# Storing the results of a fused attention and spectral-mix kernel: last rows by another queue, pair tiles by one DMA of two blocks

## The chip, the cores and the metric

One core of one Trainium2 chip. The metric is the device time of one execution, in microseconds (us); medians of several executions are quoted.

## The reference, cut to what matters

Windowed causal attention over 8 batches of 576 positions gives x (8, 576, 512). A spectral mix transforms x along the positions, multiplies 64 modes by complex weights and transforms back to y. The output is u + relu(u @ w_ch) with u = x + y, in float32: 9.44 MB.

```python
X = np.fft.rfft(x, axis=1)
Yr = einsum(Xr, w_r) - einsum(Xi, w_i); Yi = einsum(Xr, w_i) + einsum(Xi, w_r)   # 64 modes
y = np.fft.irfft(Y, n=S, axis=1)
u = x + y
return (u + np.maximum(u @ w_ch, 0.0)).astype(np.float32)
```

## The kernel before

576 rows are 4 tiles of 128 rows and one of 64. The 64 last rows of two batches share a tile of 128 partitions, the pair tile; there are four. Two whole tiles of a batch are stored together, as 128 descriptors of 4 KB (two output rows per partition). The inverse transform of batch b multiplies a table with that batch's spectrum rows (`Y`); 8 of those rows come last of all, are computed for batches 2 to 7 in one tile (`yl`), and are moved by DMA into partitions 120 to 127 of the batch's own tile.

```python
def send(b):                                    # the last 8 rows of batch b
    r0 = 2 * R + RL * (b - 2)
    nc.sync.dma_start(out=batch_tile(b)[128 - RL:].bitcast(FP32), in_=yl[r0:r0 + RL].bitcast(FP32))
...
def finish(n):                                  # last product, sum and store of tile n
    b, t = seq[n]
    add(n, "Yb", True)
    ...
    nc.vector.tensor_tensor(out=ot[:, j], in0=ps, in1=x_sb[:, b, t, :], op=ALU.add)
    if t == NT - 1:                             # the pair tile: two halves
        for i, queue in enumerate((nc.sync, nc.sync)):
            queue.dma_start(out=out[b + i, 128 * t:, :], in_=ot[64 * i:64 * i + 64, 0])
    ...
    elif j:                                     # two whole tiles
        nc.sync.dma_start(out=out[b, 128 * t - 128:128 * t + 128, :].rearrange("(p j) e -> p j e", j=2), in_=ot)
...
send(2)
turn_of = {1: 3, 3: 4, 5: 5, 7: 6, 8: 7}
for n in range(NQ):
    finish(n)
    if n in turn_of:
        send(turn_of[n])
    ...                                         # products and rectification of later tiles
```

The softmax here doesn't subtract the row's maximum and nothing guards it: scores larger than these inputs give would overflow.

## Time and profile before

| what | kernel before |
|---|---|
| time, median of 5 | 430.04 us (429.55 to 430.32) |
| last weight transfer to the first row transfer | 391.2 to 397.1 us of the span |
| stores, first packet to last | 399.2 to 426.1 us |
| VectorE's last sum ends | 420.4 us |
| span | 427.3 us |

The part to look at is small: 31 us of 427. An average over the span (DMA engines over 90% busy) says nothing about it, because the weight stream fills the rest. One reads the last slices, then stretches of some us within them, then the sync queue's own timeline. The prediction shows those lines. A packet there is one record of a DMA engine's work: one contiguous run of up to 4 KB, or a 4-byte semaphore write.

### The profile page before, as it was taken

To read this page: it belongs to the slowest core of one execution; us is meant where nothing else is said; L and a number is where in the kernel's file an instruction comes from. 1 tells how busy PE (TensorE), PEld (TensorE's weight loads), DVE (VectorE), ACT (ScalarE), POOL (GpSimd) and SP (SyncE) were. 2 spreads that over 40 slices of the span, in tenths; PEclk is the share of its full clock that TensorE was granted. 3 is DMA by queue.
4 is the path that set the end of the run, shared out by engine and by line. 5 is a ranking of instruction groups with operands and counts; after the bars stand their busy time and mean duration, and the time that the engine had idled before them with its cause. 6 is when DMAs were issued, how large, how long until landed. Compare 5 with 4: busy or idle time off the path is not lost.

```text
span 427.3 us, 11629 instructions
## 1 busy us (share of the span) xinstructions
PE 322.1 (75%) x5179; PEld 230.8 (54%) x5186; DVE 176.1 (41%) x372; ACT 164.1 (38%) x290; POOL 89.4 (21%) x171
## 2 busy tenths in 40 slices
PE   6989998998998866422488877876367685498992
PEld 5755765765665566411367666654245452266781
DVE  5566765765764200306223332221113332141993
ACT  4585765866863221001022322222012221131991
POOL 7231231241112232211221221221111122100000
PEclk9999998999996655555588998899556965589997
DMA  7999999999999999999999999999999999993698
GB/s 142 212 213 213 213 212 213 214 211 214 214 213 213 214 213 261 214 214 213 213 213 215 213 212 214 214 214 213 212 215 213 214 213 214 214 214 68 219 351 333
DMA packets 28721, 92.16 MB, mean 216 GB/s; under 512 B 2896, under 2 KB 3152, under 8 KB 28672
## 3 DMA queue, kind: packets, MB, share of 16 engines
q0 software_dynamic: 25344, 81.80, 96.1%
q1 hardware_dynamic: 3184, 9.50, 6.0%
q8 instruction: 40, 0.66, 0.6%
q10 hardware_dynamic: 144, 0.13, 0.1%
q14 instruction: 9, 0.07, 0.0%
HBM read 162.53 MB, written 9.44 MB: 402 GB/s over the span
## 4 chain that ended last, share of the span: by engine, by line
DMA 51%; PE 32%; DVE 8%; issue 4%; ACT 2%; POOL 1%; DVEq 0%; POOLq 0%
DMA wt<-in_moe_w_i_dram 45%; PE pso L316 7%; PE pst L218 6%; DMA wy<-in_moe_w_i_dram 4%; PE pso L859 4%; PE psv L235 3%; DVE x_sb L324 3%; PE pss L372 3%; PE pss L272 2%; DMA wt<-in_moe_w_r_dram 2%; PE psx L338 2%; PE pss L291 2%; DVE vT L59 2%; PE psw L709 1%; DVE ot L882 1%
## 5 line engine op out<-in xcount | busy, mean ns | idle before, releaser
L563 PE MATMUL psy<-XQ,wt 128*128 128x16 bf16 x1616 | 61.4, 191 | 72.8 <-DMA wt<-in_moe_w_i_dram 37.6
L563 PEld LDWEIGHTS <-wt 128*128 128x128 bf16 x1616 | 53.2, 103 | 87.5 <-DMA wt<-in_moe_w_i_dram 42.4
L591 DVE CAST xT<-pxt 128x256 fp32r<-128x256 bf16 (+1 forms) x68 | 26.1, 434 | 61.8 <-PE pxt L584 39.4
L115 POOL DMA_DIRECT2D wt<-in_moe_w_r_dram x54 | 29.0, 537 | 87.8 <-DMA wt<-in_moe_w_r_dram 42.2
L596 ACT CAST Z<-psz 128x512 fp32r<-128x512 f32 x36 | 21.1, 586 | 66.9 <-PE psz L594 66.6
L115 POOL DMA_DIRECT2D wt<-in_moe_w_i_dram x52 | 27.9, 536 | 84.7 <-DMA wt<-in_moe_w_i_dram 53.7
L594 PE MATMUL psz<-wch,xT 128*128 128x512 f32 x144 | 45.3, 457 | 0.0
L297 ACT ACTIVATE et<-pss 128x512 bf16<-128x512 f32 x72 | 39.2, 599 | 13.2 <-PE pss L291 13.2
L316 PE MATMUL pso<-vt,et 128*64 128x65 bf16 (+1 forms) x576 | 34.3, 210 | 5.2 <-DVE x_sb L324 5.1
L316 PEld LDWEIGHTS <-et 128*64 128x64 bf16 (+1 forms) x576 | 23.9, 114 | 17.3 <-issue 9.8
L594 PEld LDWEIGHTS psz<-wch,xT 128*128 128x128 f32 x144 | 29.2, 217 | 5.8 <-ACT Z L596 0.4
L324 DVE TENSOR_TENSOR x_sb<-pso,rcp 128x640 bf16<-128x640 f32 x32 | 26.3, 822 | 0.9
L859 PE MATMUL pso<-Y,trigI 128*128 128x512 f32 x80 | 23.1, 402 | 0.1
L59 DVE CAST YT<-psy 128x256 fp32r<-128x256 f32 x6 | 2.5, 423 | 49.4 <-PE psy L563 49.4
L882 DVE TENSOR_TENSOR ot<-pso,x_sb 128x512 f32<-128x512 f32 x35 | 22.2, 685 | 1.5 <-PE pso L859 1.1
L59 DVE CAST x_sb<-psj 128x512 bf16<-128x512 f32 x16 | 11.0, 688 | 27.2 <-PE psj L771 27.1
L58 ACT CAST YT<-psy 128x256 fp32r<-128x256 f32 x6 | 2.2, 373 | 50.7 <-DVE YT L59 50.7
L272 PE MATMUL pss<-band,ident_bf 64*64 64x512 bf16 x136 | 20.5, 414 | 1.5 <-ACT et L297 1.5
L59 DVE COPY vT<-pst 128x768 bf16<-128x768 bf16 x16 | 15.3, 957 | 13.0 <-PE pst L218 13.0
L58 ACT CAST x_sb<-psj 128x512 bf16<-128x512 f32 x16 | 9.4, 586 | 26.9 <-PE psj L771 26.9
L864 ACT ACTIVATE pso<-pso 128x512 f32<-128x512 f32 x36 | 19.1, 597 | 0.0
L859 PEld LDWEIGHTS pso<-Y,trigI 128*128 128x128 f32 x80 | 14.5, 188 | 5.5 <-ACT pso L864 1.7
(158 smaller groups left out, 496.3 us busy)
## 6 DMA issues: line engine op xcount, KB each, us to landing
wt<-in_moe_w_r_dram POOLq DMA_DIRECT2D x54, 512.0 KB, 19.1
wt<-in_moe_w_i_dram POOLq DMA_DIRECT2D x52, 512.0 KB, 19.1
out_dram<-ot SPq DMA_DIRECT2D x15, 512.0 KB, 4.2
rk<-in_k_dram POOLq DMA_DIRECT2D x8, 576.0 KB, 9.0
rq<-in_q_dram POOLq DMA_DIRECT2D x8, 576.0 KB, 12.9
rv<-in_v_dram POOLq DMA_DIRECT2D x8, 576.0 KB, 11.9
wy<-in_moe_w_r_dram POOLq DMA_DIRECT2D x3, 512.0 KB, 16.9
wy<-in_moe_w_i_dram POOLq DMA_DIRECT2D x3, 512.0 KB, 19.1
```

Source lines behind the costliest of these rows:

```text
L59: return nc.vector.tensor_copy(out=o, in_=i)
L115: nc.gpsimd.dma_start(out=wt, in_=src[m].rearrange("(p c) e -> p c e", c=NC))
L218: nc.tensor.transpose(out=ps[64 * hh:64 * hh + 64, c, :], in_=src[:, hh, (c0 + c) * D:(c0 + c + 1) * D], identity=ident_bf)
L272: nc.tensor.matmul(out=pss[(2 * w + hh) % 3][64 * half:64 * half + 64, :], lhsT=ident_bf[pp, pp], rhs=view(band[pp], 128 * half, [[0, WIN ...
L297: nc.scalar.activation(out=et[:, hh, :], in_=pss[(2 * w + hh) % 3], func=ACT_F.Exp, scale=EX_SCALE)
L316: nc.tensor.matmul(out=pso[po, hh, (i // 2) * VW:(i // 2) * VW + D + 1], lhsT=et[pk, hh, col:col + 64], rhs=vt[pk, 1 - f % 2, 2 * hh + g / ...
L324: nc.vector.tensor_tensor(out=view(x_sb, b * NT * DM + g * D, [[4 * D, 2], [DM, NT], [1, D]]), in0=view(pso, 0, [[512, 2], [VW, NT], [1, D]]),
L563: nc.tensor.matmul(out=psy[:, m % MG, e, :], lhsT=w[:, c, 128 * e:128 * e + 128], rhs=XQ[:, c, :, 1 - im:3 - im, m], start=(m % MG == im + ...
L591: nc.vector.tensor_copy(out=xT[:, :, w * k:w * k + w], in_=view(psts[k], j, [[128, NC], [n, w]]))
L594: nc.tensor.matmul(out=psz, lhsT=xT[:, c, :], rhs=wch[:, c, :], start=(c == 0), stop=(c == NC - 1))
L859: nc.tensor.matmul(out=tps[n], lhsT=trigI[:, tr:tr + 128], rhs=pair_tile(what, bb), start=False, stop=stop and r0 + k == 128, skip_group_c ...
L882: nc.vector.tensor_tensor(out=ot[:, j], in0=ps, in1=x_sb[:, b, t, :], op=ALU.add)
```

## The change

Its intent: the sync queue alternates stores with row transfers and falls behind. Five of the six row transfers go to GpSimd, which is idle by then, and all are issued at once. A pair tile, which took two issues, is stored by one.

```diff
-            nc.sync.dma_start(out=batch_tile(b)[128 - RL:].bitcast(FP32), in_=yl[r0:r0 + RL].bitcast(FP32))
+            queue = nc.sync if b == 2 else nc.gpsimd
+            queue.dma_start(out=batch_tile(b)[128 - RL:].bitcast(FP32), in_=yl[r0:r0 + RL].bitcast(FP32))
@@
-                for i, queue in enumerate((nc.sync, nc.sync)):
-                    queue.dma_start(out=out[b + i, 128 * t:, :], in_=ot[64 * i:64 * i + 64, 0])
+                nc.sync.dma_start(out=out[b:b + 2, 128 * t:, :], in_=ot[:, 0])
@@
-        send(2)
-        turn_of = {1: 3, 3: 4, 5: 5, 7: 6, 8: 7}
+        for b in range(2, B):
+            send(b)
         for n in range(NQ):
             finish(n)
-            if n in turn_of:
-                send(turn_of[n])
```

## The prediction

> **What bounds the kernel now.** I read the page's slices first, to find the stage that the change touches. One slice is 10.7 us.
>
> ```profile
> span 427.3 us, 11629 instructions
> ...
> DMA  7999999999999999999999999999999999993698
> GB/s 142 212 213 213 213 212 213 214 211 214 214 213 213 214 213 261 214 214 213 213 213 215 213 212 214 214 214 213 212 215 213 214 213 214 214 214 68 219 351 333
> ```
>
> For 36 slices the time is the weight stream from memory. The change starts after it, in the last 31 us, where 9.44 MB of results are stored; there the bytes per us are at their highest. I split that stage by stretches (PE, PEld, DVE, ACT, POOL busy with counts, granted clock, DMA share, GB/s), and looked at when VectorE makes the results.
>
> ```profile
> 399.00:403.00 4.00, 4.00 (x19) 3.12 (x18) 3.62 (x7) 4.00 (x10) 0.00 (x0) 1.00 0.94 330
> 403.00:407.00 4.00, 4.00 (x19) 3.27 (x18) 3.70 (x6) 4.00 (x10) 0.00 (x0) 1.00 0.85 301
> 411.00:415.00 4.00, 4.00 (x19) 3.21 (x18) 3.58 (x7) 3.98 (x9) 0.00 (x0) 1.00 1.03 411
> 419.00:423.00 4.00, 0.10 (x1) 0.00 (x0) 1.39 (x4) 0.00 (x0) 0.00 (x0) 0.87 1.00 378
> 423.00:427.30 4.30, 0.00 (x0) 0.00 (x0) 0.00 (x0) 0.00 (x0) 0.00 (x0) 0.50 0.68 255
> ```
>
> ```profile
> 419.65 0.74 DVE L879 TENSOR_TENSOR ot<-pso,x_sb 128x256 f32<-128x256 f32 x2
> ```
>
> VectorE is done at 420.4, but stores run on to 426.1 (end of the last packet in the trace's packet records) and the span ends at 427.3. So the last 7 us are stores alone: the end is set by the DMA engines. At 411 to 415 they are saturated: 411 GB/s over 16 engines is 25.7 GB/s each, which is 159 ns for a 4096-byte packet, and the packet records have just that median (2048 bytes: 84 ns, 1024 bytes: 46 ns, the 4-byte semaphore write: 9 ns). But at 399 to 407 they move only 301 to 330. The sync queue's timeline says why.
>
> ```profile
> 398.86 0.69 SPq L848 DMA_DIRECT2D Y<-yl  x1
> 399.60 0.42 SPq L890 DMA_DIRECT2D out_dram<-ot  x1
> 400.14 0.65 SPq L848 DMA_DIRECT2D Y<-yl  x1
> 400.85 0.63 SPq L890 DMA_DIRECT2D out_dram<-ot  x1
> 401.52 0.65 SPq L848 DMA_DIRECT2D Y<-yl  x1
> 402.22 0.88 SPq L890 DMA_DIRECT2D out_dram<-ot  x1
> 403.26 0.65 SPq L848 DMA_DIRECT2D Y<-yl  x1
> 404.02 1.42 SPq L885 DMA_DIRECT2D out_dram<-ot  x2
> ```
>
> Here the queue is busy back to back, alternating a small row transfer (8 rows of 4 KB) with a store, and stores go out late: the second pair is ready when VectorE's fourth sum ends at about 398.84 and is issued at 399.60; the first pair tile (line 885, two halves of 64 rows) is ready at about 402.4 and is issued at 404.02. That early loss is never made up, since the engines are then full. Last, how many engines a transfer uses:
>
> ```profile
> q1 hardware_dynamic: 3184, 9.50, 6.0%
> q10 hardware_dynamic: 144, 0.13, 0.1%
> ```
>
> If a store uses 16 engines it leaves one 4-byte semaphore packet on each. 15 x (128+16) for the whole stores, 8 x (64+16) for the half ones, 2 x (128+16) for the last two on this queue and 6 x (8+8) for the rows make 2160 + 640 + 288 + 96 = 3184, the page's count exactly. So 128 rows and 64 rows go over 16 engines, and 8 rows over 8 engines.
>
> **What the Trainium skill says.** (1) "DMA: Bandwidth & Descriptors", section "Why a DMA increments its semaphore by 16 and not by 1": the number of engines k is the largest one up to 16 that divides the slowest dimension (not 1) of both access patterns, and from a hardware queue the lowest-numbered k engines are taken. The packet count above agrees for 128, 64 and 8 rows; which engines they were, the packet records do not tell. (2) The same page, "Rules for kernel authors": an outermost dimension below 16 confines the whole DMA to at most that many engines. (3) The same section of rules says that two transfers to disjoint partition halves are not worth it and to use one of 128 partitions; that is what the change seems to aim at. (4) "Perfetto Trace Analysis", section "DMA Instruction — HWDGE (DVE, Sync)": the reported time of an issue includes making its descriptors, and an engine's descriptor buffer can fill. The trace agrees: a whole store's issue takes 0.37 us when little is queued (406.3) and up to 1.17 us from 410 on.
>
> **The change part by part.** The PE, VectorE and ScalarE orders are the same in both built programs; only the queues differ.
>
> Part A, the rows. Five of six row transfers (0.65 to 0.69 us each, about 3.3 us) leave the sync queue; GpSimd issues them, having nothing to do since its last weight issue at 372.0 (its issues there take 0.53 us). Stores would then go out when ready: 398.85 instead of 399.60, 402.45 instead of 404.02. By itself this fills the gap at 399 to 407. VectorE makes a 512 KB pair in about 1.36 us (35 sums and two halves from 396.07 to 420.39, 36 tiles, 0.676 us each), and the engines move one in 1.28 us (8 packets of 159 ns and a semaphore write). So the engines would keep up, and end soon after the last sum. The least time from issue to landing that the trace has for any store is 2.9 us; from the ScalarE issue at 420.43 that gives 423.3, plus 1.2 us from last packet to end: 424.5, or 2.8 us saved.
>
> Part B, the pair tiles. Eight issues become four; some 4 us less of sync queue, but much of their 0.58 to 1.31 us is waiting for room and no gain. The point is the pattern. In the built program the destination is (2 blocks) x (64 rows) x 512, the source 128 partitions x 512: slowest dimensions 2 and 128, so k = 2. All 128 packets of 2 KB go to two engines, 64 each: 64 x 84 ns + 9 ns = 5.4 us, where before each engine had 8 packets (about 0.7 us). Packets of one queue on one engine run in turn, so the engines' shares of later stores wait behind.
>
> Now I add up the load of those two engines. Issue to first packet is 1.1 us (397.94 to about 399.05). The first four stores keep them busy to about 404.1 (issued at 397.94, 398.85, 400.05 and 401.65; the last one's packets start at 402.8 and take 1.28). The first pair tile is issued at about 402.45, so its packets are queued by then, and from here the two engines never run dry:
> - 4 pair tiles x 5.39 = 21.5 us
> - 11 whole stores x 1.28 = 14.1 us
> - the 256 KB store 8 x 84 + 9 ns = 0.7 us, and the two of 128 KB 2 x (8 x 46 + 9 ns) = 0.75 us
>
> Sum 37.1 us, so the last packet ends at 441.2 instead of 426.1: +15.1 us. The 1.2 us to the end stays. 430.04 + 15.1 = 445.1 us. The other 14 engines will have long idle stretches. The sync queue will be stuck issuing pair tiles, as their 65 descriptors per engine are far above the about 24 per engine that seem to be open when issues stall now (an estimate: packets issued less packets done, some 360 to 415 at the ends of stalled issues, over 16). VectorE may then wait for a free output buffer (7 of them), but that costs nothing beyond, as the two engines have work all the time.
>
> **The rivals.**
> 1. The store is spread over 16 engines after all (the pattern rearranged on the way to the hardware). For it: nothing in this trace shows a two-block pattern. Against it: the skill's rule, which fits three row counts here. Then part A alone counts: 427 us, within 2%.
> 2. Two engines, but faster when they have the memory to themselves. Against it: the packet time is 159 ns also at 399 to 403, where the engines move 330 instead of 411 GB/s, so it is the engine's own speed. 10% faster 2 KB packets would make 443.
> 3. Two engines, with gaps: if the queue is blocked for the whole transfer and the next store's descriptors arrive 1.1 us after it, each pair tile adds up to that: 4 x 1.1, about 449.
> 4. GpSimd's rows come late and hold up the matrix products of batches 3 to 7. Five issues of 0.53 us from about 397.1 end near 400; batch 3 is first used by the products at about 402, after two more sums than batch 2. Even 1 or 2 us would be hidden behind part B.
>
> **Range and chances.** I give k = 2 about 0.88. The loads then make 441 to 449. With k = 16, about 427. Predicted 445, range 440.5 to 449.5; slower 0.87 (over 438.6), same 0.12, faster 0.01.
>
> **What would show it.** Packets on the sync queue: 2984 if each pair tile leaves 128 + 2 (2160 + 288 + 16 + 520), 3040 if 128 + 16. Issue to landing of the pair tiles at 6 us or more, against 3.5 now; long issues on their line and on the next; the DMA share of the tail near 0.6 instead of 0.9; bytes per us falling towards 50 GB/s where only two engines work. Wrong would be: pair tiles landing in 3 to 4 us with the tail at 400 GB/s, or a wait of matrix products for the GpSimd rows.

## The result, and the profile after

446.27 us (445.97 to 446.41, 5 runs) against 430.04 (429.55 to 430.32, 5 runs): slower, ratio 1.0378, 95% interval 1.0363 to 1.0393. Ratios here are the mean time of one kernel's runs over the mean of the other's runs of the same rounds, so not quite the ratio of the medians.

The page of the kernel after, the slices and the sync queue's packets (one slice is 11.1 us):

```profile
span 443.7 us, 11621 instructions
...
DMA  8999999999999999999999999999999999918654
GB/s 143 212 213 213 213 213 213 213 213 215 213 209 213 212 228 246 214 213 215 213 214 213 214 213 214 213 213 214 213 213 214 212 214 213 192 34 296 217 199 147
...
q1 hardware_dynamic: 2984, 9.34, 6.0%
```

Before, the DMA share in the last four slices was 3, 6, 9, 8; now it falls from 8 to 6, 5, 4. The sync queue has 2984 packets, which is the count for two engines per pair tile (128 + 2) and not for 16 (3040). The same stage in stretches (columns as in the prediction: length, busy time of five engines, granted clock, DMA share, GB/s):

```profile
399.00:403.00 4.00, 3.75 (x17) 2.67 (x16) 3.18 (x6) 3.93 (x9) 0.91 (x2) 1.00 0.96 311
407.00:411.00 4.00, 4.00 (x19) 3.24 (x18) 3.16 (x6) 4.00 (x10) 0.00 (x0) 1.00 0.62 176
415.00:419.00 4.00, 2.89 (x12) 1.72 (x10) 1.25 (x2) 2.08 (x5) 0.00 (x0) 1.00 0.94 307
419.00:423.00 4.00, 1.59 (x7) 1.29 (x8) 2.37 (x4) 2.16 (x4) 0.00 (x0) 0.99 0.42 168
423.00:427.00 4.00, 2.39 (x6) 1.13 (x4) 3.38 (x6) 1.16 (x2) 0.00 (x0) 0.50 0.62 211
435.00:439.00 4.00, 0.00 (x0) 0.00 (x0) 0.00 (x0) 0.00 (x0) 0.00 (x0) 0.50 0.46 166
```

Full stretches (307 GB/s) alternate with empty ones (168), and the matrix engine (the first column), which was busy for 4.00 of 4 us up to 419 before, is down to 2.89 at 415 and to 1.59 at 419. A finer view cuts 397 to 444 us into 40 slices of 1.2 us:

```profile
GB/s 0 101 345 276 335 401 397 319 303 258 138 54 54 213 340 329 307 232 371 129 56 254 387 282 70 51 51 56 234 349 350 344 316 274 51 56 49 52 31 0
...
out_dram<-ot SPq DMA_DIRECT2D x15, 512.0 KB, 10.4
```

There is a floor of 49 to 56 GB/s that comes back with each pair tile. A 2048-byte packet takes 84 ns, but starts a little before the one ahead of it ends: in the third tile one begins every 80 ns on each of two engines, which makes 51 GB/s. Whole stores, which do use 16 engines, land after 10.4 us instead of 4.2 (median), because two of their sixteen shares wait behind a pair tile. The sync queue's timeline:

```profile
397.99 4.40 SPq L890 DMA_DIRECT2D out_dram<-ot  x4
402.98 0.60 SPq L885 DMA_DIRECT2D out_dram<-ot  x1
...
406.44 0.53 SPq L885 DMA_DIRECT2D out_dram<-ot  x1
407.74 8.59 SPq L890 DMA_DIRECT2D out_dram<-ot  x4
416.42 0.52 SPq L885 DMA_DIRECT2D out_dram<-ot  x1
417.04 5.63 SPq L890 DMA_DIRECT2D out_dram<-ot  x2
...
423.97 7.90 SPq L890 DMA_DIRECT2D out_dram<-ot  x3
```

The pair tiles themselves (line 885) are issued in 0.5 to 1.1 us. The store after the first of them is quick too (0.51 us when the merged lines are split); it is the store after the second, the third and the fourth that takes long (4.55, 4.65 and 5.91 us). When the second tile had been issued, at 406.97, the first one's packets had hardly begun (405.90, 12 of 128 done). So the queue took in two pair tiles with two stores between them, and blocked at the next store. Who waits, for whom, in us, times and longest (from 391 us on):

```profile
DVE ot L883 <- DMA out_dram<-ot: 8.2, 3, 3.8
...
PEld pso L860 <- DMA Y<-yl: 0.7, 1, 0.7
...
PE pso L860 <- DMA Y<-yl: 0.2, 1, 0.2
```

VectorE runs out of output buffers for 8.2 us in all. And the matrix products wait for the rows of batch 2, which they did not before. The last two lines are one wait, for the weight load and for the product that follows it, and must not be added; the timeline has both ending at 400.57:

```profile
400.57 0.54 PEld L860 LDWEIGHTS pso<-Y,trigI 128*128 128x128 f32 x3 [0.69 <-DMA Y<-yl]
400.57 0.97 PE L860 MATMUL pso<-Y,trigI 128*128 128x512 f32 x3 [0.25 <-DMA Y<-yl]
```

So it is 0.7 us at most, and the products themselves stand still for 0.25.

### The profile page after: what moved, and what is told of

It is laid out like the page before. It is cut to its first block, busy times and chain, and to the rows that moved or that the text cites. A ratio compares the mean times of both kernels' runs of the same rounds, so it can differ in the third digit from the quotient of the medians.

```text
span 443.7 us, 11621 instructions
## 1 busy us (share of the span) xinstructions
PE 329.3 (74%) x5186; PEld 234.4 (53%) x5186; DVE 177.1 (40%) x372; ACT 164.7 (37%) x290; POOL 91.8 (21%) x176
## 3 DMA queue, kind: packets, MB, share of 16 engines
q1 hardware_dynamic: 2984, 9.34, 6.0%
## 4 chain that ended last, share of the span: by engine, by line
DMA 57%; PE 29%; DVE 7%; issue 2%; ACT 2%; POOL 0%; DVEq 0%; POOLq 0%; SPq 0%
DMA wt<-in_moe_w_i_dram 34%; DMA wt<-in_moe_w_r_dram 9%; PE pso L316 6%; PE pst L218 5%; DMA out_dram<-ot 5%; DMA wy<-in_moe_w_i_dram 4%; DMA wch<-in_moe_w_ch_dram 4%; PE psv L235 3%; PE psx L338 3%; DVE x_sb L324 3%; PE pss L372 3%; PE pss L272 2%; PE pss L291 2%; DVE vT L59 2%; PE psy L563 1%
## 5 line engine op out<-in xcount | busy, mean ns | idle before, releaser
L594 PE MATMUL psz<-wch,xT 128*128 128x512 f32 x144 | 49.0, 486 | 0.0
L594 PEld LDWEIGHTS psz<-wch,xT 128*128 128x128 f32 x144 | 31.4, 233 | 6.5 <-ACT Z L596 0.4
## 6 DMA issues: line engine op xcount, KB each, us to landing
out_dram<-ot SPq DMA_DIRECT2D x15, 512.0 KB, 10.4
```

The lines of the kernel that those rows point to most:

```text
L594: nc.tensor.matmul(out=psz, lhsT=xT[:, c, :], rhs=wch[:, c, :], start=(c == 0), stop=(c == NC - 1))
```

## The experiments

Four questions: which part of the change costs the time; is it the number of engines or something else about one DMA over two blocks; why do the rows on GpSimd bring nothing; and is there a version that beats both. The kernel before, run beside them on the same chips, had medians of 429.80 to 430.05 us.

**Rows alone** (the change with the two half stores put back).

```diff
-                nc.sync.dma_start(out=out[b:b + 2, 128 * t:, :], in_=ot[:, 0])
+                for i, queue in enumerate((nc.sync, nc.sync)):
+                    queue.dma_start(out=out[b + i, 128 * t:, :], in_=ot[64 * i:64 * i + 64, 0])
```

> Rows by GpSimd as in the change, pair tiles in two halves as before. Two-engine theory: none of the loss is here; the stores go out when ready, so 426 to 429 us (up to 1% below the kernel before), 3040 + 160 - ... in packets: sync queue 15x144 + 2x144 + 8x80 + 16 = 3104. Rival (the GpSimd rows come late and hold up the products): 435 us or more, with waits of the matrix products for the rows.

Measured: 429.58 us, ratio 1.0006 (0.9985 to 1.0027), correct; 3104 packets. No loss is here, but no gain either, where the prediction had counted 2.8 us. (Of the packet counts in the text on record, the last one is the expectation.) Its profiled execution took 432.66 us, with the 3 us lost earlier, in the weight stream; so I read its trace from the first row transfer on. The products wait 0.8 us for rows.

**Pair tiles alone** (the kernel before with the one DMA of two blocks).

> Pair tiles in one DMA each as in the change, all rows by the sync queue as before. Two-engine theory: all of the loss is here; 446 to 450 us, at least as slow as the whole change, since rows behind a blocked sync queue can only be later. Rival (rows): 429 to 431 us, as the kernel before.

Measured: 447.01 us, ratio 1.0396 (1.0382 to 1.0409). All of the loss is in the pair tiles.

**Rows first.** Same packets, same sizes, same two blocks of the output; only the order in which the destination is walked differs. Results of the pair tiles are wrong.

```diff
-                nc.sync.dma_start(out=out[b:b + 2, 128 * t:, :], in_=ot[:, 0])
+                nc.sync.dma_start(out=out[b:b + 2, 128 * t:, :].rearrange("i p e -> p i e"), in_=ot[:, 0])
```

> The whole change, but the destination of the pair tile's one DMA is walked rows first, blocks second (64 x 2 x 512 instead of 2 x 64 x 512): the same 128 packets of 2 KB to the same 128 rows of the output, in another order, so the pair-tile rows are wrong on purpose. Two-engine theory: the slowest dimensions 64 and 128 allow 16 engines, 128 + 16 packets per pair tile (3040 on the sync queue), landing in 3 to 5 us, time 425.5 to 428.5 us. Rival (one DMA that hops between two blocks is slow as such, or the packets of 2 KB are): 440 us or more, as the whole change.

Measured: 428.21 us, ratio 0.9961 (0.9949 to 0.9973); 3040 packets on the sync queue:

```profile
q1 hardware_dynamic: 3040, 9.34, 5.6%
```

Exchanging the two outer dimensions takes 18 us off the changed kernel. That rules out the two blocks, the packet size and the single issue as causes.

**Only the last pair tile in one DMA.**

```diff
+                if b == B - 2:
+                    nc.sync.dma_start(out=out[b:b + 2, 128 * t:, :], in_=ot[:, 0])
+                else:
+                    for i in range(2):
+                        nc.sync.dma_start(out=out[b + i, 128 * t:, :], in_=ot[64 * i:64 * i + 64, 0])
```

> Rows by GpSimd; only the last of the four pair tiles in one DMA of two blocks, the other three in halves. Two-engine theory: one tile puts 5.4 - 0.7 = 4.7 us more on the two engines with little after it to hide it, so the kernel with rows alone + 4.7 us, 430 to 434 us. Rival (a loss that needs several blocked stores, such as the output buffers running out): within 1 us of the kernel with rows alone.

Measured: 433.71 us, ratio 1.0093 (1.0079 to 1.0108). That is 4.1 us over the kernel with rows alone, against 4.7 expected. One tile costs about a quarter of the whole, so the loss does not need several of them.

**Halves walked in 2 or 4 outer steps.** Two DMAs per pair tile, as before, but the destination of each has an outermost count of 2 (or 4). Row order wrong.

```diff
-                    queue.dma_start(out=out[b + i, 128 * t:, :], in_=ot[64 * i:64 * i + 64, 0])
+                    to = out[b + i, 128 * t:, :].rearrange("(p q) e -> q p e", q=2)   # and q=4
+                    queue.dma_start(out=to, in_=ot[64 * i:64 * i + 64, 0])
```

> Rows by GpSimd, pair tiles in two halves as before, but each half's destination is walked in 2 outer steps (even rows, then odd ones; rows wrong on purpose). Two-engine theory: 2 engines for each half, 2992 packets on the sync queue (15x144 + 2x144 + 16 + 8x66), and the same load on the same two engines as in the change: 444.5 to 447.5 us. Rival (it is the one DMA over two blocks that is slow): 429 to 431 us.

> The same with 4 outer steps per half. Two-engine theory, as a rule of the outermost count: 4 engines for each half, 3008 packets. From the first packet to the last, a busy engine in the change takes 43.5 us, of which 42.2 are its load (15 whole stores x 1.28, 4 tiles x 5.39, 1.45 for the last three); with four engines the load is 15 x 1.28 + 4 x 2 x (16 x 84 + 9 ns) + 1.45 = 31.5 us, so 32.8 us with the same 1.3 idle, against 27.0 in the kernel with rows alone: + 5.8 us, 434 to 437 us. Rival (any outer count below 16 falls onto a slow path of its own): 444 us or more.

Measured: 447.79 us with 2 outer steps (ratio 1.0416, 1.0400 to 1.0431; 2992 packets), 0.3 us above the range expected, and 438.50 with 4 (1.0208, 1.0171 to 1.0244; 437.15 to 440.55 us; 3008 packets). The packet counts are those of 2 and 4 engines. In the view of 40 slices from 397 us on, the floor doubles with the count; first 2 outer steps, then 4:

```profile
GB/s 0 56 341 282 338 410 354 295 208 338 102 44 52 164 367 344 374 382 146 52 52 108 370 370 85 41 52 54 326 360 356 368 291 74 54 51 38 23 0 0
```

```profile
GB/s 0 0 152 356 320 332 311 418 328 129 193 367 410 213 98 109 242 399 422 406 406 295 78 80 231 389 393 143 94 289 355 392 395 406 318 122 54 8 0 8
```

41 to 54 against some 78 to 109 GB/s. So the rule is one of the outermost count, and two separate halves do not help. The size with 4 engines was missed: 34.96 us from the first packet to the last where I expected 32.8 (load 31.5), so 3.5 us came on top of the load and not 1.3. Why is open. Idle engines do not show: between 409 and 432 fewer than four packets were under way for only 0.6% of the time.

**Rows by the sync queue, pair tile rows first** (the kernel before with the rows-first store, wrong).

> The kernel before, with the pair tile's two halves made one DMA walked rows first (16 engines; pair-tile rows wrong on purpose), all rows still by the sync queue. If a half of 64 partitions is slow as such (its 2 KB packets in the kernel before took up to 168 ns and more in the slowest twentieth, against 93 with one DMA of 128 partitions), this saves what the same step saved beside the GpSimd rows, 1.0 to 1.6 us: 428.3 to 429.0 us, and the packets of 2 KB take 84 to 95 ns. Rival (the saving came only from the fewer issues on a freed sync queue): within 0.5 us of the kernel before.

Measured: 429.10 us (428.71 to 430.60), ratio 0.9983 (0.9968 to 0.9998), just outside the range expected. 95% of its 2 KB packets take 92 ns or less; in the kernel before the same mark is at 168 ns. Summed and spread over 16 engines, its 2 KB packets take 0.7 us less each. So two stores of 64 partitions are slower than one of 128, and part of the saving does not need the GpSimd rows. (The four issues fewer came with it; the run does not separate them.)

**Earlier rows, and later GpSimd transfers.** Two edits to the rows-first kernel ask whether the new wait for rows matters. The first makes ScalarE's copy of the last rows one step earlier (`if n == 2` becomes `if n == 1`). The second has GpSimd copy 112x512 values before its row transfers:

```diff
+        lag = yp.tile([128, DM], FP32, name="lag")
+        nc.gpsimd.tensor_copy(out=lag[0:NR], in_=yl[0:NR, 0].bitcast(FP32))
```

> The wrong kernel with the rows-first walk, and ScalarE's copy of the last rows one rectification earlier. The rows of batch 2 then land about 0.55 us earlier, and the matrix products' wait for them (1.0 us) shrinks by so much; the third sum is 0.5 us later. If the wait for the rows holds up the end: 427.4 to 428.0 us. If the end is set by the stores alone: 428.2 us, as without.

> The wrong kernel with the rows-first walk, and a copy of 112x512 on GpSimd before its row transfers, so that they start some 0.6 to 1 us after the sync queue's. If GpSimd's transfers, by going first on the same engines, delay the rows of batch 2: the matrix products' wait for those rows (1.0 us) is 0.4 us or less, 427.4 to 428.1 us. Rival (those rows take 3.4 us to land by the sync queue in any company): the wait stays at 0.9 to 1.1 us and the time at 428.2.

Measured: 428.20 us (ratio 0.9957, 0.9945 to 0.9969) and 428.44 (0.9965, 0.9953 to 0.9977), both as the rows-first kernel. The second is a little above the 428.1 that the text gave if GpSimd's transfers delay those rows. (That text's wait of 1.0 us is again two waits that overlap; it was 0.7.) In both the matrix products no longer wait for rows at all. With the lag, the sync queue's transfer was issued just as before and was in time, so the wait did come from GpSimd's transfers going beside it: in the packet records the sync queue's first row packet begins 1.41 us after its issue with the lag and 1.78 without, after GpSimd's first. But although VectorE's last sum then ends 23.3 us after the first row transfer instead of 23.8 (lag), the end does not move: it is set by the stores.

**Interleaved pair tile.** To make the rows-first walk right, the 128 partitions of a pair tile alternate between the two batches: table columns alternate with zeros, and four permuting products reorder x in the stage that waits for weights. The store is the rows-first one. The edit is cut here to two places.

```diff
+            nc.tensor.matmul(out=psj, lhsT=ident_pair, rhs=x_sb[:, b, NT - 1, :], start=True, stop=True)
+            evac(x_sb[:, b, NT - 1, :], psj, b % 4)
@@
-                tr = 128 * t + (64 - r0 if t == NT - 1 else 0)
+                tr = 128 * t + (r0 == 0 if t == NT - 1 else 0)     # table at odd columns from 513, zeros between
```

> The change with the pair tile laid out so that its 128 partitions alternate between the two batches; the one DMA of 64 x 2 rows is then right. Costs four more matrix products and four more evictions of 128x512 in the stage that waits for weights. Two-engine theory: correct, and as fast as the wrong kernel with that walk, 427.5 to 429 us, 0.3 to 0.6% below the kernel before. Rival (the extra work shows): 430 us or more.

Measured: correct, 428.72 us (428.41 to 428.88), ratio 0.9970 (0.9958 to 0.9982). It beats the kernel before by 0.3%, which is small but clear of the interval, and the changed one by 17.5 us.

## Why the prediction was right

**What bounds the stage: right.** The DMA engines set the end before and after; removing waits of the compute engines (the two edits above) moved nothing.

**Two engines per pair tile: right.** 2984 packets; a floor of 49 to 56 GB/s; and swapping the two outer dimensions brings the time back. The packet records show it directly: from 426.0 to 429.5, with the third tile alone, two packets are under way for 90% of the time and three for 10% (where one starts before the last has ended), never another number. That the two engines are the lowest-numbered ones is not shown, as the records do not name the engine. That it is the same two for each tile and for their share of the whole stores follows from the load, next.

**The load: right in its sum, late in its start.** Predicted 37.1 us from the start of the first pair tile's packets to the last packet. The packet records have 405.90 to 442.44 us, 36.5; each tile's 128 packets take 5.2 to 6.1 us from first to last, where 5.4 was worked out. Between the tiles lie 2.47, 4.96 and 2.46 us, in which 2, 4 and 2 whole stores were due, at 1.24 us each (8 packets, of which one begins every 154 ns where the two engines work alone, and a semaphore write). So the two engines took tiles and stores in the order of their issue, without a gap.

The start was predicted at 404.1, and it was 1.8 us later. The step that was off is the first four stores, which were to keep the engines busy to about 404.1. Their packets ran back to back from 399.27 to 405.82, which is 6.5 us where 4 x 1.28 = 5.1 were counted: the packets of the first two took 174 and 189 ns in the mean, not 159. The row transfers, which the sum left out, go on in the same stretch: GpSimd's 40 packets take 15.4 us in all, up to 1.07 us each. That these slowed the stores is not shown. The stores were also issued somewhat later (the fourth at 402.06 instead of 401.65, after the products' wait for rows), but this cost nothing: the fourth one's packets began 2.15 us after its issue, when the third's were ending. So the last packet came at 442.4 instead of 441.2, and the time at 446.27 instead of 445.1.

**One sign was wrong.** The working had the queue stuck at the pair tiles, with about 24 descriptors per engine open. The tiles were issued in 0.52 to 1.10 us, so the long issues came on the next line only; and by 406.97 some 140 were open on each of the two engines (an estimate: 116 packets of the first tile and the second tile's 128, over two, with two stores' 9 each and the tiles' semaphores). The profile gives no landing for the tiles; the first one's last packet ended 9.0 us after its issue, so the sign of 6 us or more fits. Queue and VectorE did stand still later, and as the working said, that cost nothing beyond, since the two engines had work all the time.

**Part A: the term that was mis-sized.** The working gave it 2.8 us by itself; alone it brought 0.3 (429.58 against 429.91), which is within noise. The step that failed is that the engines would "keep up" at 1.28 us per 512 KB. That holds for stores of 128 partitions, not for halves of 64. The same three stretches, from 2, 10 and 22 us after the first row transfer, of the kernel before, with rows alone, and with rows and the rows-first store; the last stretch is left out:

```profile
399.10:407.10 8.00, 8.00 (x36) 6.43 (x36) 7.31 (x13) 8.00 (x17) 0.00 (x0) 1.00 0.89 315
407.10:419.10 12.00, 12.00 (x50) 8.95 (x48) 11.37 (x20) 11.43 (x23) 0.00 (x0) 1.00 0.99 377
```

```profile
402.20:410.20 8.00, 7.61 (x33) 5.91 (x33) 6.75 (x11) 7.58 (x16) 0.76 (x2) 1.00 1.00 354
410.20:422.20 12.00, 12.00 (x52) 9.26 (x50) 11.37 (x20) 11.98 (x25) 0.00 (x0) 1.00 1.01 373
```

```profile
399.20:407.20 8.00, 7.75 (x33) 6.01 (x33) 6.87 (x12) 7.70 (x16) 0.82 (x2) 1.00 1.00 364
407.20:419.20 12.00, 12.00 (x51) 9.20 (x50) 11.37 (x20) 11.98 (x24) 0.00 (x0) 1.00 1.02 405
```

GpSimd rows do fill the early gap (315 to 354), as predicted. But in the middle the engines show a share of 1.0 and move only 373 to 377 as long as there are halves, and 405 without: they are busy and slow. The Trainium skill has this, in "SBUF — State Buffer", section "Can I just issue two DMAs to hit both halves?": only one transfer that spans all 128 partitions reaches all 16 ports. The packet times agree (168 against 93 ns at the 95% mark); that the ports are the reason, no run here shows. I had read the halves' 16 engines from the packet count and not asked how fast those engines could read. The 2.8 us were also too high for another reason: even the rows-first kernel, with both faults gone, saves 1.7 us.

**The rivals.** 16 engines: refuted by the packet count. Faster packets on two engines: no, the median stays at 84 ns. Gaps between: none from the first tile on; from 405.9 to 442.4 fewer than two packets are under way for 0.1% of the time. (The 1.3 us called idle in a text, 43.5 against a load of 42.2, lie before the first tile.) Late rows: those of batch 2, by the sync queue, did come late, by up to 0.7 us, and were hidden.

**The lucky part.** The total of +16.2 us against +15.1 predicted hides that the pair tiles cost less over the kernel with rows alone (16.7 by the medians, 446.27 - 429.58, of different rounds) than the working had it (17.9), and the rows gave less. The two errors have opposite signs.

## What to carry to other kernels

Before joining two stores into one, write down the outermost dimension of both access patterns: it is what spreads the transfer over the DMA engines, and 2 there means 2 engines, however large the transfer. Check it with the packet count of the sync queue, where every engine in use left a semaphore packet (GpSimd's queue counts otherwise: its five transfers of 8 rows left 160 packets). One transfer of all 128 partitions is still better than two halves, if the destination can be walked with a long dimension outermost; it may be worth laying out the tile so that this walk is the right one.

## What the Trainium skill lacked or had wrong

- "DMA: Bandwidth & Descriptors", rules for kernel authors: the advice to use one 128-partition transfer in place of two disjoint halves stands without the condition that the other side's outermost dimension must be long too. Followed with two blocks outermost it made this kernel 3.8% slower (446.27 us); with the 64 rows outermost it saves (428.21). The condition is in another row of the same table.
- The same page gives about 27 GiB/s per engine, which is 29 GB/s. Here a 4096-byte packet takes 159 ns at the median in every run, 25.8 GB/s; where the two engines work alone (437.7 to 441.3 in the changed kernel), one begins every 154 ns on each, 26.6 GB/s.
- "Perfetto Trace Analysis", HWDGE section: it says that a descriptor buffer can fill, but not how much is queued before an issue blocks. Here pair tiles with 65 packets on each of two engines were issued in 0.5 to 1.1 us, the second while the first had hardly begun, and the store behind the second, third and fourth took 4.55 to 5.91 us.
- No page has the size of the delay that transfers by GpSimd give to one of the sync queue that is issued beside them: the sync queue's first row packet came 1.78 us after its issue instead of 1.41 when GpSimd's were started later, and the products that needed those rows waited up to 0.7 us instead of not at all.
